# Normalization of v moved to VectorE behind a power on GpSimd, with query weights, biases and loads moved in the order of work (linear attention, then a gated MLP)

## The chip, the cores and the metric

The kernel runs on one core of one Trainium2 chip. The metric is the device time of one execution in microseconds (us), the median of several executions. Five engines work side by side, each through its own queue in its own order, and wait for each other by semaphores: TensorE (PE in the profile; its weight loads are PEld), VectorE (DVE), ScalarE (ACT), GpSimd (POOL) and SyncE (SP, which here only issues DMAs).

## What is computed

The inputs are q, k and v of 8 batches, 8 heads, 576 tokens and 64 elements a head, and the weights of a feature map and of an MLP. Cut to what matters:

```python
def phi(x):                                   # 64 -> 256 features
    proj = einsum('bhsd,df->bhsf', x, w_phi)  # 128 projections
    proj = proj - max(abs(proj), axis=-1)
    return concatenate([exp(proj), exp(-proj)])
kv  = einsum('bhsf,bhsd->bhfd', phi(k), v);  z = sum(phi(k), axis=2)
x   = (phi(q) @ kv) / (phi(q) @ z + 1e-06)    # -> (batch, 576, 512)
h   = maximum(x @ w_in, 0.0);  u, v = h[..., :512], h[..., 512:]
v_n = (v - mean(v)) / sqrt(var(v) + 1e-06)    # over the 512 of a token
v_s = einsum('ts,bsd->btd', w_spatial, v_n) + b_spatial[None, :, None]
out = (u * v_s) @ w_out
```

The normalization of v is the line of `v_n`: a mean and a variance for each token, then one subtraction and one product for each element.

## The kernel before

**Units and batches.** The 576 tokens of a batch are 512 main tokens, four blocks of 128, and a tail of 64; the tails of two batches share a tile. Attention works in 36 units: for each batch four *pair* units (two heads, all main tokens), and for each two batches one *tail* unit (all heads, 128 tail tokens). Unit 2 is the first tail; units 0, 1, 3 and 4 are batch 0, 5 to 8 batch 1, 9 the second tail, 10 to 13 batch 2.

**A unit's stages** are spread over several steps. `a_keys` projects the keys (L267), VectorE takes their absolute maximum `mk` (L279) and ScalarE two exponentials (L282). `a_scale` (L299) scales v by the exponential of the maximum: two products of 128x512 on GpSimd (`vs`, L307) and a small copy; tails do the same into `vst` (`tail_scale`, L317). `a_queries` takes the queries' maxima `mq` (L293) and splits them into two bf16 halves, `mhl` (L296, L297), on VectorE for the first five units and on GpSimd later. `a_max_t` transposes `mhl` (L328), `a_qfeat` projects the queries again, now with the maximum subtracted inside the product, and takes exponentials (L366). From batch 2 on (`merged`, XB = 2) the subtraction sits in the weights: `wm` (L161) holds the projection of each head beside rows of `sel` that pick the head's maximum, and `a_max_t` writes the maxima into free rows of the transposed queries (L331, L332). `a_kv` and `a_num` make the sums and the numerator.

**The MLP** of a batch is a list of tasks (`b_tasks`, L592) that is queued when the batch's attention is done, and is interleaved with later units by `fill` (L620), a given cost per step. `b_v` makes a block of v (L448), ScalarE its relu `vr` (L450), VectorE mean and variance (L451, L452). `root` (L454) takes four small GpSimd instructions: epsilon added, the power -0.5 (`ALU.pow`), mean times that, and the sign. `normalize` (L464) then does one product and one addition with two numbers per token on GpSimd: four times 128x512 a batch (`b_ln`, L481) and once 64x512 for the tail, inside `b_v_tail`. `b_u` makes u, `b_s` (L519) the spatial products with `w_spT` (L524, L525), which VectorE multiplies by u (L527), `b_o` the output. `w_spT` is made once, by transposes of the loaded `wsp`, `wspr` and `wspt` among batch 0's tasks (`transpose_spatial`, L210); after the last of them ScalarE copies the bias from `bsp_row` into two rows of it.

**The order.** A planner places instructions on each engine as their inputs come ready by its own estimate. What is wrapped in `pin` (L60) keeps its place behind what the program has given the same engine just before. The profile names pinned instructions by L61, the line of `pin`. The loop over steps (L713) emits step i's stages and MLP tasks and then what `at(i, ...)` has listed for step i: the loads (k, q and MLP weights from GpSimd's queue, with a cast to bf16; v from SP's), the transposing DMAs of keys and queries (`cross`, on SP, three steps ahead of a unit of batch 2 or later), the copy `q_even`, the tail scaling of batch 1, and `weights_with_max`, which builds `wm` in twelve small GpSimd instructions in steps 6 and 7.

Of the kernel before, what the change touches and what calls it, by code (L numbers as in the profile page):

```python
# [16 lines left out]
def kernel(  # L17
# [162 lines left out]
        pin(nc.scalar.copy)(out=wphi2[r, y * F:(y + 1) * F], in_=wphi_f[r, :])  # L180
    for i in range(2):
        fill_vnt(i, nc.gpsimd.tensor_copy)
    for x in ("k", "q"):
        pin(nc.gpsimd.tensor_copy)(out=half_tile(x, 0, 0)[:, 2:4], in_=first[x, 2])
    load("k", 0, 1, 0, 2)
# [5 lines left out]

    w_in_bf = cpool.tile([P, KC, DFF], BF16)
    w_out_bf = cpool.tile([P, KC, DM], BF16)
    wsp = s2.tile([P, NB, T0], BF16, tag="vn", name="wsp", bufs=2)
    wspr = cpool.tile([P, NB, TL], BF16)
    wspt = s2.tile([TL, S], BF16, tag="ob", name="wspt", bufs=6)
    bsp_row = s2.tile([P, S], FP32, tag="xT", name="bsp_row", bufs=3)
    nc.sync.dma_start(out=bsp_row[TL:TL + 1, :], in_=moe_b_spatial)
# [11 lines left out]
    def transpose_spatial(i):  # L210

        pt = psum.tile([P, S], BF16, tag="bank", name="pt")
        if i < NB:
            sc = POS[i]
            for tp, c in enumerate(POS):
                nc.tensor.transpose(out=pt[:, tp * P:(tp + 1) * P], in_=wsp[:, c, bass.ds(sc, P, step=NB)],
                                    identity=ident)
            nc.tensor.transpose(out=pt[:, T0:S], in_=wspt[:, bass.ds(sc, P, step=NB)],
                                identity=ident[:TL, :TL])
            nc.vector.tensor_copy(out=w_spT[:, i, :], in_=pt)  # L220
            return
        for bl in range(2):
            lo = bl * TL
            for tp, c in enumerate(POS):
                nc.tensor.transpose(out=pt[lo:lo + TL, tp * P:(tp + 1) * P], in_=wspr[:, c, :], identity=ident)
            nc.tensor.transpose(out=pt[lo:lo + TL, T0:S], in_=wspt[:, T0:S], identity=ident[:TL, :TL])
            nc.vector.tensor_copy(out=w_spT[lo:lo + TL, NB + bl, :], in_=pt[lo:lo + TL, :])
        for bl, row in ((0, TL), (1, 0)):
            r = slice(row, row + 1)
            pin(nc.scalar.copy)(  # L230
                out=w_spT[r, NB + bl, 0:T0].rearrange("o (a b p) -> o a b p", a=2, b=2),
                in_=bsp_row[r, 0:T0].rearrange("o (p b a) -> o a b p", a=2, b=2))
            pin(nc.scalar.copy)(out=w_spT[r, NB + bl, T0:S], in_=bsp_row[r, T0:S])


    def merged(u):
        return u["pair"] and u["b"] >= XB

    def weights_with_max(n):
        for j in range(4 * n, 4 * n + 4, 2):  # L240
            pin(nc.gpsimd.tensor_copy)(out=wm[:, j, :], in_=wphi2[:, 0:F])
            pin(nc.gpsimd.tensor_tensor)(out=wm[:, j + 1, :], in0=wphi2[:, F:2 * F], in1=sel[:, j + 1, :], op=ALU.add)
            pin(nc.gpsimd.tensor_copy)(out=wm[D:D + 2 * H, j, :], in_=sel[0:2 * H, j, :])

    def q_even(u):
        u["qE"] = qts[u["i"] % len(qts)]
# [37 lines left out]
    def a_queries(u):  # L284

        m, early = mhl[u["i"] % NM], u["i"] < EARLY
        if not early:
            mq = small.tile([P, H], FP32, tag="mq", name="mq")
        for half in range(2):
            pq = by_token(u["qT"], half)  # L290
            if early and half == 0:
                mq = pq[:, 0, 0:H]
            nc.vector.tensor_reduce(out=mq[:, 4 * half:4 * half + 4], in_=pq, axis=AX.X, op=ALU.max,  # L293
                                    apply_absolute_value=True)
        eng = nc.vector if early else nc.gpsimd
        eng.tensor_copy(out=m[:, 0:H], in_=mq)  # L296
        eng.tensor_tensor(out=m[:, H:2 * H], in0=mq, in1=m[:, 0:H], op=ALU.subtract)  # L297

    def a_scale(u):  # L299
        em = small.tile([P, 2, H], FP32, tag="em" if u["pair"] else "em_t", name="em", bufs=3 if u["pair"] else 1)  # L300
        for s, sc in ((0, -1.0), (1, 1.0)):
            nc.scalar.activation(out=em[:, s, :], in_=u["mk"], func=AF.Exp, bias=0.0, scale=sc)  # L302
        if u["pair"]:
            pj = u["pj"]
            vs = feat.tile([P, 2, H, DA], BF16, tag="vs", name="vs", bufs=4)
            for s in range(2):
                nc.gpsimd.tensor_tensor(out=vs[:, s, :, 0:D], in0=st[u["b"]]["v"][:, pj * H:(pj + 1) * H, :],  # L307
                                        in1=em[:, s, :].unsqueeze(2).to_broadcast([P, H, D]), op=ALU.mult)
            nc.gpsimd.tensor_copy(out=vs[:, :, :, D:DA], in_=em.unsqueeze(3).to_broadcast([P, 2, H, 2]))
            u["vs"] = vs  # L310
        else:
            d = gs[u["g"]]
            d["vs"], d["unit"], d["em"] = vst[u["g"] % 2], u, em
            for bl in range(2 if u["g"] else 1):
                tail_scale(u["g"], bl)
# [135 lines left out]
        nc.vector.bn_stats(out=stats[r], in_=dst[r])  # L451
        nc.vector.bn_aggr(out=mv[r], in_=stats[r])  # L452

    def root(mv, r, n):  # L454

        var = small.tile([P, NB, 1], FP32, tag="var", name="var")
        rs = small.tile([P, NB, 2], FP32, tag="rs", name="rs")
        nc.gpsimd.tensor_scalar(out=var[r, 0:n], in0=mv[r, 0:n, 1:2], scalar1=1e-6, scalar2=None, op0=ALU.add)
        nc.gpsimd.tensor_tensor(out=rs[r, 0:n, 0:1], in0=var[r, 0:n], in1=neghalf[r, 0:n].unsqueeze(2), op=ALU.pow)
        nc.gpsimd.tensor_tensor(out=var[r, 0:n], in0=mv[r, 0:n, 0:1], in1=rs[r, 0:n, 0:1], op=ALU.mult)  # L460
        nc.gpsimd.tensor_scalar(out=rs[r, 0:n, 1:2], in0=var[r, 0:n], scalar1=-1.0, scalar2=None, op0=ALU.mult)
        return rs

    def normalize(dst, src, rs):  # L464
        nc.gpsimd.tensor_scalar(out=dst, in0=src, scalar1=rs[:, 0:1], scalar2=rs[:, 1:2],  # L465
                                op0=ALU.mult, op1=ALU.add)

    def b_v(b, j):
        d = st[b]
        if j == 0:  # L470
            d["vn"] = s2.tile([P, NB, HALF], BF16, tag="vn", name="vn", bufs=2)
            d["mv"] = small.tile([P, NB, 2], FP32, tag="mv", name="mv")
            d["vr"] = {}
        d["vr"][j] = s2.tile([P, HALF], BF16, tag="vr", name="vr", bufs=5)
        stats = small.tile([P, 6], FP32, tag="stats", name="stats")
        v_mm(lambda kc: d["xT"][:, kc, j * P:(j + 1) * P], d["vr"][j], slice(0, P), stats, d["mv"][:, j, :])

    def b_root(b):
        st[b]["rs"] = root(st[b]["mv"], slice(0, P), NB)

    def b_ln(b, j):  # L481
        d = st[b]
        normalize(d["vn"][:, j, :], d["vr"][j], d["rs"][:, j, :])

    def b_v_tail(g, bls):
        d = gs[g]
# [2 lines left out]
        stats = small.tile([P, 6], FP32, tag="stats", name="stats")  # L489
        mv = small.tile([P, 1, 2], FP32, tag="mv_t", name="mv_t")  # L490
        v_mm(lambda kc: d["xTt"][:, kc, r], vr, r, stats, mv[:, 0, :])
        rstd = root(mv, r, 1)
        for bl in bls:
            r = slice(bl * TL, (bl + 1) * TL)
            normalize(vnt[g % 2][r, bl, :], vr[r], rstd[r, 0, :])

    def b_u(b, dc):
        d = st[b]
# [93 lines left out]
    def b_tasks(b):  # L592
# [5 lines left out]
        ss = [(MS, lambda dc=dc: b_s(b, dc)) for dc in range(KC)]  # L598
        ns = [(0.0, lambda j=j: b_ln(b, j)) for j in range(NB)]
        ts = outs[:1] + [(MM, lambda: b_v_tail(g, [bl]))] + vs[:2] + outs[1:2] + vs[2:]  # L600
        ts.append((0.0, lambda: b_root(b)))
        if b == 0:
            ts += [(0.3, lambda i=i: transpose_spatial(i)) for i in range(NB + 1)]
        for y in range(NB):
            ts += ns[y:y + 1] + outs[2 + y:3 + y] + us[y:y + 1]
        ts += [(MM / 2, lambda: b_u_tail(g, [bl]))] + ss
        ts.append((MS / 2, lambda: b_s_tail(g, [bl])))
        return ts + (out_tasks(b) if b == B - 1 else [])
# [70 lines left out]
        io.setdefault(i, []).append(lambda: f(*a))  # L679

    at(1, load_v, 1)
    at(2, load, "k", 1, 0)
    at(2, load, "q", 1, 0)
    at(3, load, "k", 1, 1)
    at(3, load, "q", 1, 1)
    at(4, load_weight, w_in_bf[:, :, HALF:DFF], cols[:, :, HALF:DFF])
    at(4, load_weight, wspt, moe_w_spatial[T0:S, :])
    at(5, tail_scale, 0, 1)
    at(5, load_weight, wsp, rows[:, :, 0:T0])
    at(5, load_weight, wspr, rows[:, :, T0:S])  # L690
    at(6, load_weight, w_in_bf[:, :, 0:HALF], cols[:, :, 0:HALF])
    at(8, load_weight, w_out_bf, moe_w_out.rearrange("(kc p) f -> p kc f", p=P))
    for u in units:
        i = u["i"]
        if not u["pair"] and u["g"] > 0:
            early = 1 if u["g"] > 1 else 0
            at(i - AT - early, load_tail, "k", u["g"])
            for x in ("q", "v"):
                at(i - AT + 1 - early, load_tail, x, u["g"])
        if u["pair"] and u["b"] >= XB:  # L700
            if u["pj"] == 0:
                for n, (x, y) in enumerate((("k", 0), ("q", 0), ("k", 1), ("q", 1))):
                    at((4, 4, 6, 7)[n] if u["b"] == XB else i - AB + n, load, x, u["b"], y)
                for y in range(2):
                    at(i - AB + 1 + 2 * y, load_v, u["b"], y)
            for x in ("k", "q"):
                at(i - XP, cross, x, u)
    at(6, weights_with_max, 0)
    at(7, weights_with_max, 1)
    for u in units:  # L710
        if merged(u):
            at(u["i"] - 1, q_even, u)
# [36 lines left out]
```

## Time and profile before

| what | value |
|---|---|
| median of 3 executions | 283.72 us (282.17 to 284.65) |
| profiled execution, its own time | 284.76 us |
| span of the profiled execution | 282.7 us, 8134 instructions |
| granted TensorE clock, mean | 0.986 |
| `vs` products on GpSimd (L307) | 64, mean 1044 ns, 65.5 us |
| normalization on GpSimd (L465), 128x512 and 64x512 | 32 and 8, mean 766 and 767 ns |
| power on GpSimd (L459), 128x4 and 64x1 | 8 and 8, mean 1046 and 584 ns |
| the other steps of `root` (L458, L460, L461), 128x4 | 236, 203 and 248 ns |
| the same, 64x1 | 239, 186 and 250 ns |
| `wm` on GpSimd: copies of 128x128, additions, copies of 16x128 | 4 each, 297, 426 and 283 ns |
| bias copies on ScalarE, 1x512 and 1x64 | 2 each, 1111 and 238 ns |
| small operations on VectorE: reciprocal 128x4, memset 128x5 | 163 and 62 ns |
| ScalarE copy 128x512 bf16 (L262) | 615 ns |

In a row of busy times by stage the columns are the stage, its length, and for each engine its busy time with the number of instructions, then the granted share of TensorE's clock, the mean busy share of the DMA engines (transfers waiting in a queue count, so it can be over 1) and GB/s. A row of waits gives the engine, its instruction and line, what it waited for, the total, how often, and the longest. A row of the chain gives start, duration, and the instruction. A matmul's duration holds its way through the array; four of 512 columns that follow each other take 0.86 us of the chain.

### The profile page before, as it was taken

What the parts mean: (1) busy time and instruction counts of PE and PEld (TensorE: products, weight loads), DVE (VectorE), ACT (ScalarE), POOL (GpSimd) and SP (SyncE); (2) the same over time, 40 slices, a digit from 0 to 9 for tenths busy, and PEclk for the clock granted to TensorE, in tenths of its full rate; (3) what the DMA queues carried; (4) which work ended last, traced back from release to release, by engine and by line L of the source; (5) the groups of instructions that cost most, each with busy time, mean ns of one, the idle gap of its engine ahead of it and who ended that gap; (6) DMA issues with size and microseconds to landing.
All of it is one profiled execution on the core that took longest, in us unless ns stands there. A gap on an engine that the chain in (4) does not pass through costs nothing.

```text
span 282.7 us, 8134 instructions
## 1 busy us (share of the span) xinstructions
PE 257.1 (91%) x3001; PEld 173.1 (61%) x3042; DVE 231.2 (82%) x576; ACT 219.5 (78%) x499; POOL 200.5 (71%) x362
## 2 busy tenths in 40 slices
PE   2777979986999999999999999999999999999993
PEld 1466866754776667666666775766666765654441
DVE  7979987875799979998889989998889897566341
ACT  5689996978399997899889987899699977723601
POOL 5988999999859886799949974889548832511710
PEclk9979999999799999999999999999999999999999
DMA  7989999999986999989989999999766301120305
GB/s 205 238 205 125 152 144 217 111 164 195 225 87 163 130 243 196 162 206 210 214 96 130 207 252 138 200 214 217 86 122 132 86 2 68 46 77 37 112 3 186
DMA packets 85148, 42.43 MB, mean 150 GB/s; under 512 B 52146, under 2 KB 80498, under 8 KB 85108
## 3 DMA queue, kind: packets, MB, share of 16 engines
q1 hardware_dynamic: 60020, 30.95, 55.0%
q0 software_dynamic: 24928, 10.89, 34.9%
q8 instruction: 24, 0.39, 0.6%
q14 instruction: 16, 0.13, 0.2%
q10 hardware_dynamic: 160, 0.07, 0.1%
HBM read 32.85 MB, written 9.44 MB: 150 GB/s over the span
## 4 chain that ended last, share of the span: by engine, by line
PE 62%; POOL 12%; ACT 9%; DVE 6%; DMA 4%; issue 4%; SPq 0%; POOLq 0%; ACTq 0%; DVEq 0%
PE ps L524 9%; PE pv L448 9%; PE po L549 9%; PE ps L267 6%; PE pu L503 6%; ACT kf L282 5%; PE pv L379 4%; PE pn L399 4%; PE pq L345 3%; DMA q_bf<-in_q_dram 3%; PE ps L525 2%; POOL vs L307 2%; POOL vst L61 2%; DVE stats L451 2%; ACT qf L366 2%
## 5 line engine op out<-in xcount | busy, mean ns | idle before, releaser
L282 ACT ACTIVATE kf<-ps 128x512 bf16<-128x512 f32 x144 | 76.2, 637 | 9.9 <-DVE mk L279 9.5
L307 POOL TENSOR_TENSOR vs<-v_f,em 128x512 bf16<-128x512 f32 x64 | 65.5, 1044 | 19.0 <-ACT em L302 17.6
L366 ACT ACTIVATE qf<-pq 128x512 bf16<-128x512 f32 x128 | 66.6, 620 | 9.6 <-PE pq L345 8.5
L279 DVE TENSOR_REDUCE mk<-ps 128x4 f32<-128x512 f32 x72 | 47.7, 677 | 1.2 <-PE ps L267 0.5
L293 DVE TENSOR_REDUCE mq<-ps 128x4 f32<-128x512 f32 x62 | 39.8, 680 | 2.6 <-PE ps L267 1.4
L524 PE MATMUL ps<-w_spT,vn 128*128 128x512 bf16 x116 | 33.1, 384 | 3.6 <-POOL vn L465 3.1
L527 DVE TENSOR_TENSOR uT<-ps,uT 128x512 bf16<-128x512 f32 x32 | 22.0, 687 | 16.8 <-PE ps L525 16.8
L451 DVE BATCH_NORM_STATS2 stats<-vr 128x6 f32<-128x512 bf16 (+1 forms) x40 | 26.7, 684 | 7.3 <-ACT vr L450 6.9
L549 PE MATMUL po<-w_out_bf,uT 128*128 128x512 bf16 x121 | 32.0, 380 | 0.4
L503 PE MATMUL pu<-xT,w_in_bf 128*128 128x512 bf16 x121 | 31.5, 380 | 0.5 <-issue 0.2
L448 PE MATMUL pv<-w_in_bf,xT 128*128 128x512 bf16 x116 | 30.7, 380 | 0.7
L450 ACT ACTIVATE vr<-pv 128x512 bf16<-128x512 f32 (+1 forms) x40 | 23.5, 615 | 7.6 <-PE pv L448 5.9
L379 PE MATMUL pv<-vs,kf 128*128 128x66 bf16 x512 | 24.3, 194 | 1.3 <-ACT kf L282 1.3
L390 DVE TENSOR_TENSOR x<-pn,rc 128x256 bf16<-128x256 f32 x64 | 24.9, 417 | 0.3
L465 POOL TENSOR_SCALAR vn<-vr,rs 128x512 bf16<-128x512 bf16 x32 | 24.3, 766 | 1.1
L399 PEld LDWEIGHTS <-qf 128*128 128x128 bf16 x512 | 20.5, 99 | 7.1 <-issue 1.4
L505 ACT ACTIVATE uT<-pu 128x512 bf16<-128x512 f32 x32 | 19.7, 641 | 4.9 <-PE pu L503 3.2
L379 PEld LDWEIGHTS <-kf 128*128 128x128 bf16 x512 | 21.8, 97 | 2.5 <-issue 1.5
L552 ACT COPY ob<-po 128x512 f32<-128x512 f32 x18 | 11.0, 614 | 14.9 <-PE po L549 8.4
L399 PE MATMUL pn<-kv,qf 128*128 128x66 bf16 x512 | 22.0, 195 | 0.3 <-ACT qf L366 0.3
L381 PE MATMUL pv<-vst,kf 128*128 128x66 bf16 x128 | 21.2, 192 | 0.0
L524 PEld LDWEIGHTS <-vn 128*128 128x128 bf16 x128 | 11.7, 98 | 13.8 <-POOL vn L465 4.6
(133 smaller groups left out, 572.2 us busy)
## 6 DMA issues: line engine op xcount, KB each, us to landing
out_dram<-ob SPq DMA_DIRECT2D x32, 256.0 KB, 2.5
v_f<-in_v_dram SPq DMA_DIRECT2D x14, 512.0 KB, 7.0
k_bf<-in_k_dram POOLq DMA_DIRECT2D x14, 256.0 KB, 6.3
q_bf<-in_q_dram POOLq DMA_DIRECT2D x14, 256.0 KB, 6.4
qt<-qT_b SPq DMA_DIRECT2D x24, 64.0 KB, 4.2
v_tl<-in_v_dram SPq DMA_DIRECT2D x8, 128.0 KB, 3.4
v_f<-in_v_dram SPq DMA_DIRECT2D x1, 1024.0 KB, 9.4
w_in_bf<-in_moe_w_in_dram POOLq DMA_DIRECT2D x2, 512.0 KB, 10.5
```

Source lines behind the costliest of these rows:

```text
L279: nc.vector.tensor_reduce(out=u["mk"][:, hs], in_=pk, axis=AX.X, op=ALU.max, apply_absolute_value=True)
L282: nc.scalar.activation(out=u["kf"][:, s, hs, :], in_=pk, func=AF.Exp, bias=0.0, scale=sc)
L293: nc.vector.tensor_reduce(out=mq[:, 4 * half:4 * half + 4], in_=pq, axis=AX.X, op=ALU.max, apply_absolute_value=True)
L307: nc.gpsimd.tensor_tensor(out=vs[:, s, :, 0:D], in0=st[u["b"]]["v"][:, pj * H:(pj + 1) * H, :], in1=em[:, s, :].unsqueeze(2).to_broadcast( ...
L366: nc.scalar.activation(out=qf[:, s], in_=pq, func=AF.Exp, bias=0.0, scale=sc)
L379: nc.tensor.matmul(out=pv[:, hh, s, :], lhsT=u["kf"][:, s, 4 * hh + c, :], rhs=u["vs"][:, s, 4 * hh + c, :], start=(c == 0), stop=False)
L399: nc.tensor.matmul(out=pn[:, pos, :], lhsT=u["qf"][hh][:, s, pos, :], rhs=d["kv"][:, 2 * u["pj"] + hh, s, :], start=(s == 0), stop=(s == 1))
L448: nc.tensor.matmul(out=pv[r], lhsT=lhs(kc), rhs=w_in_bf[:, kc, HALF:DFF], start=(kc == 0), stop=(kc == KC - 1))
L451: nc.vector.bn_stats(out=stats[r], in_=dst[r])
L503: nc.tensor.matmul(out=pu, lhsT=w_in_bf[:, kc, dc * P:(dc + 1) * P], rhs=d["xT"][:, kc, :], start=(kc == 0), stop=(kc == KC - 1))
L524: nc.tensor.matmul(out=ps, lhsT=d["vn"][:, sp, cs], rhs=w_spT[:, sp, 0:T0], start=(sp == 0), stop=False)
L549: nc.tensor.matmul(out=po[r], lhsT=lhs(dc), rhs=w_out_bf[:, dc, :], start=(dc == 0), stop=(dc == KC - 1))
```

## The change

- `normalize` runs on VectorE as one instruction (the mean subtracted, then the product with the root), pinned. Epsilon is added on VectorE right after the last statistics (`with_eps`); `root` is then the power alone, on GpSimd, pinned. The product with the mean and the sign are gone.
- Root and normalization are tasks of their own for tail and main blocks. The tail's root comes right behind the last `b_v`, the main blocks' root behind the first `b_u`; the tail's and the first block's normalization come behind the second `b_u`, two more behind the third, the last behind the fourth.
- `wm` is built before step 0, in two ScalarE copies and one GpSimd addition over all heads.
- The four bias copies on ScalarE move from the last `transpose_spatial` to steps 1 and 2.
- Loads: `wsp` and `wspr` become one load of whole rows. The two query loads of batch 2 move from steps 4 and 7 to 7 and 9, the second key load from 6 to 8, its v loads from 5 and 7 to 8 and 9; `wsp` from 5 to 7, `wspt` from 4 to 6, the second half of `w_in` from 6 to 5, `w_out` from 8 to 9; the second tail's loads from 4 and 5 to 5 and 6; batch 3's k and q loads come one step later.
- `mhl`, `vs` and its small copy are pinned.

```diff
+    pin(nc.scalar.copy)(out=alternate(wm, 0), in_=wphi2[:, 0:F].unsqueeze(1).to_broadcast([P, NP, F]))
+    pin(nc.scalar.copy)(out=alternate(wm[D:D + 2 * H], 0), in_=alternate(sel[0:2 * H], 0))
+    pin(nc.gpsimd.tensor_tensor)(out=alternate(wm, 1), in0=alternate(sel, 1),
+                                 in1=wphi2[:, F:2 * F].unsqueeze(1).to_broadcast([P, NP, F]), op=ALU.add)
...
-    wsp = s2.tile([P, NB, T0], BF16, tag="vn", name="wsp", bufs=2)
-    wspr = cpool.tile([P, NB, TL], BF16)
+    wsp = s2.tile([P, NB, S], BF16, tag="vn", name="wsp", bufs=2)
...
-        for bl, row in ((0, TL), (1, 0)):
-            r = slice(row, row + 1)
-            pin(nc.scalar.copy)(
+    def spatial_bias(bl):
+        r = slice(TL, TL + 1) if bl == 0 else slice(0, 1)
+        pin(nc.scalar.copy)(
...
-        eng.tensor_copy(out=m[:, 0:H], in_=mq)
-        eng.tensor_tensor(out=m[:, H:2 * H], in0=mq, in1=m[:, 0:H], op=ALU.subtract)
+        pin(eng.tensor_copy)(out=m[:, 0:H], in_=mq)
+        pin(eng.tensor_tensor)(out=m[:, H:2 * H], in0=mq, in1=m[:, 0:H], op=ALU.subtract)
...
-    def root(mv, r, n):
-        var = small.tile([P, NB, 1], FP32, tag="var", name="var")
-        rs = small.tile([P, NB, 2], FP32, tag="rs", name="rs")
-        nc.gpsimd.tensor_scalar(out=var[r, 0:n], in0=mv[r, 0:n, 1:2], scalar1=1e-6, scalar2=None, op0=ALU.add)
-        nc.gpsimd.tensor_tensor(out=rs[r, 0:n, 0:1], in0=var[r, 0:n], in1=neghalf[r, 0:n].unsqueeze(2), op=ALU.pow)
-        nc.gpsimd.tensor_tensor(out=var[r, 0:n], in0=mv[r, 0:n, 0:1], in1=rs[r, 0:n, 0:1], op=ALU.mult)
-        nc.gpsimd.tensor_scalar(out=rs[r, 0:n, 1:2], in0=var[r, 0:n], scalar1=-1.0, scalar2=None, op0=ALU.mult)
+    def with_eps(mv, r, n):
+        var = small.tile([P, NB, 1], FP32, tag="var", name="var")
+        nc.vector.tensor_scalar(out=var[r, 0:n], in0=mv[r, 0:n, 1:2], scalar1=1e-6, scalar2=None, op0=ALU.add)
+        return var
+
+    def root(var, r, n):
+        rs = small.tile([P, NB, 1], FP32, tag="rs", name="rs")
+        pin(nc.gpsimd.tensor_tensor)(out=rs[r, 0:n], in0=var[r, 0:n], in1=neghalf[r, 0:n].unsqueeze(2), op=ALU.pow)
         return rs
 
-    def normalize(dst, src, rs):
-        nc.gpsimd.tensor_scalar(out=dst, in0=src, scalar1=rs[:, 0:1], scalar2=rs[:, 1:2],
-                                op0=ALU.mult, op1=ALU.add)
+    def normalize(dst, src, mv, rs):
+        pin(nc.vector.tensor_scalar)(out=dst, in0=src, scalar1=mv[:, 0:1], scalar2=rs, op0=ALU.subtract, op1=ALU.mult)
...
-        ts.append((0.0, lambda: b_root(b)))
+        ts.append((0.0, lambda: b_root_tail(g, [bl])))
         if b == 0:
             ts += [(0.3, lambda i=i: transpose_spatial(i)) for i in range(NB + 1)]
-        for y in range(NB):
-            ts += ns[y:y + 1] + outs[2 + y:3 + y] + us[y:y + 1]
+        ns.insert(0, (0.0, lambda: b_ln_tail(g, [bl])))
+        ts += outs[2:3] + us[:1] + [(0.0, lambda: b_root(b))] + outs[3:4] + us[1:2]
+        ts += ns[:2] + outs[4:] + us[2:3] + ns[2:4] + us[3:] + ns[4:]
...
+    at(1, spatial_bias, 0)
+    at(2, spatial_bias, 1)
...
+    at(4, load, "k", 2, 0)
     at(5, tail_scale, 0, 1)
-    at(5, load_weight, wsp, rows[:, :, 0:T0])
-    at(5, load_weight, wspr, rows[:, :, T0:S])
-    at(6, load_weight, w_in_bf[:, :, 0:HALF], cols[:, :, 0:HALF])
-    at(8, load_weight, w_out_bf, moe_w_out.rearrange("(kc p) f -> p kc f", p=P))
+    at(5, load_weight, w_in_bf[:, :, 0:HALF], cols[:, :, 0:HALF])
+    at(5, load_tail, "k", 1)
+    at(6, load_tail, "v", 1)
+    at(6, load_tail, "q", 1)
+    at(6, load_weight, wspt, moe_w_spatial[T0:S, :])
+    at(7, load, "q", 2, 0)
+    at(7, load_weight, wsp, rows)
+    at(8, load, "k", 2, 1)
+    at(8, load_v, 2, 0)
+    at(9, load, "q", 2, 1)
+    at(9, load_v, 2, 1)
+    at(9, load_weight, w_out_bf, moe_w_out.rearrange("(kc p) f -> p kc f", p=P))
...
-    at(6, weights_with_max, 0)
-    at(7, weights_with_max, 1)
```

## The prediction

> **What bounds the kernel now.** I read the totals first, then engine busy time by stage, then who waits for whom in each stage, then the chain.
>
> ```profile
> PE 257.1 (91%) x3001; PEld 173.1 (61%) x3042; DVE 231.2 (82%) x576; ACT 219.5 (78%) x499; POOL 200.5 (71%) x362
> PEclk9979999999799999999999999999999999999999
> ```
>
> No engine is idle enough to be ruled out by its total, so the stages have to be looked at. The second line shows two dips of the granted clock, in the third and the eleventh slice.
>
> ```profile
> core 0: us, PE busy (x) PEld busy (x) DVE busy (x) ACT busy (x) POOL busy (x), PEclk, DMA share, GB/s
> 28.00:77.00 49.00, 42.69 (x567) 31.96 (x571) 38.60 (x104) 39.55 (x93) 46.42 (x86) 0.97 1.31 172
> 105.00:210.00 105.00, 103.76 (x1239) 69.94 (x1257) 95.03 (x225) 91.87 (x214) 80.36 (x145) 1.00 1.10 178
> 210.00:255.00 45.00, 44.02 (x512) 28.21 (x517) 35.56 (x95) 32.71 (x74) 21.98 (x42) 1.00 0.29 68
> 70.20:73.60 3.40, 3.38 (x36) 2.40 (x37) 2.15 (x8) 0.00 (x0) 3.31 (x7) 0.50 1.29 285
> ```
>
> From 28 to 77 us POOL is busy 46.4 of 49 us: it is the bound. From 105 to 210 PE is busy throughout and DVE 95.0 of 105 us. From 210 on only PE is full. The last row is the second dip: 3.4 us at half clock. TensorE's and VectorE's waits tell what those loads mean:
>
> ```profile
> PE ps L524 <- POOL vn L465: 2.4, 2, 1.3
> PE pt L328 <- POOL mhl L297: 1.5, 1, 1.5
> PE ps L267 <- ACT qf L366: 1.1, 1, 1.1
> ...
> DVE uT L527 <- PE ps L525: 4.3, 6, 1.2
> DVE qT_b L331 <- PE pt L328: 2.1, 2, 1.2
> ```
>
> The first three are PE's in 28 to 77, the last two DVE's in 105 to 210, where all of DVE's named waits sum to 8.3 us (4.3+2.1+1.1+0.8). The chain shows what the first row stands for, and the timeline of the end shows it again:
>
> ```profile
> 66.25 0.77 POOL vn L465
> 67.02 0.82 POOL q_bf L61
> 67.90 2.28 POOL vn L465 x3
> 70.22 0.61 PE ps L524
> ...
> 264.56 1.04 POOL L459 TENSOR_TENSOR rs<-var,neghalf 128x4 f32<-128x4 f32 x1
> 266.31 3.02 POOL L465 TENSOR_SCALAR vn<-vr,rs 128x512 bf16<-128x512 bf16 x4
> 267.65 0.63 PE L524 MATMUL ps<-w_spT,vn 128*128 128x512 bf16 x2
> 269.38 0.39 PE L524 MATMUL ps<-w_spT,vn 128*128 128x512 bf16 x1 [0.36 <-POOL vn L465]
> ```
>
> Both times the spatial products stand behind GpSimd's normalization. What the same work may cost on VectorE:
>
> ```profile
> L332 DVE COPY qt<-qT_b x24: 283/285/1564, 77.1 to 239.7; 16x512 bf16<-16x512 bf16 x24
> L465 POOL TENSOR_SCALAR vn<-vr,rs x32: 757/767/796, 66.3 to 268.6; 128x512 bf16<-128x512 bf16 x32
> L451 DVE BATCH_NORM_STATS2 stats<-vr 128x6 f32<-128x512 bf16 x32 | 21.4, 683 | 3.5 <-ACT vr L450 3.1
> ```
>
> The minimum and maximum of the first row matter: the copy of 1564 ns, at 166.71 us, ran while GpSimd did its two `vs` products from 166.07 to 168.12; the copy ended with them.
>
> **The change part by part.** The sums are against the profiled execution (284.76 us, span 282.7); the median of the three runs is 1.04 us lower, and I apply the differences to the median, 283.7.
>
> *Normalization in the middle.* GpSimd loses per batch four products of 0.767, one of 0.767 for the tail and three of four small steps, twice (0.69 and 0.68): 5.2 us. It was not waited for there, so this brings nothing by itself. VectorE gains five normalizations and two additions of epsilon. No row shows this operation on VectorE; 0.285 (the copy of as many bf16 elements in SBUF) and 0.683 (statistics over the same tile) bound it. I take 0.285, since the copy too reads and writes SBUF alone. For the addition the nearest rows are 0.062 (a memset of 128x5) and 0.163 (the reciprocal of 128x4); I take 0.1. That is 5 x 0.285 + 2 x 0.1 = 1.63 us a batch. On top come waits for GpSimd: the 24 copies took 9.7 us where 24 x 0.285 is 6.8, so 0.12 each on average; `vs` and `vst` fill about a third of GpSimd's time there (8 x 1.04 a batch and 2 x 1.04 for the tail, of about 30), which would make a random start wait a third of some 0.9 (half a pair), about 0.3. Between these 0.2: 1.0 us a batch. The normalizations are pinned behind the power on GpSimd (1.05 us, 0.58 for the tail), which stands in GpSimd's order behind `vs` products; if it is late, the `mk` and `mq` reductions queued behind on VectorE are late and with them ScalarE's exponentials: 0 to 1.05 a batch, I take 0.2. Together 2.8 us a batch, against DVE's named idle time of 8.3 us over the 3.5 batches of 105 to 210, 2.4 a batch. So most is absorbed and VectorE is then full. About 4.6 batches lie between 80 and 215 us; I take a loss of 0.5 in each, **+2.3**. Bounds: 0, if idle time takes all, and 4.6 x 2.8 = 13 if none. Later batches cost nothing: DVE has 9.4 of 45 us free from 210 on.
>
> A rule speaks against this part: by the Trainium skill, "SBUF — State Buffer", section Who interferes with whom, a Vector operation that uses two ports and a GpSimd instruction exclude each other for the whole instruction. The row of 1564 ns agrees, the median of 285 says that it seldom happens; by the rule every start into a `vs` pair waits, about 0.3 each, 0.5 a batch more than I take.
>
> *The start.* GpSimd's 46.4 us in 28 to 77 lose the first batch's normalization (5.2) and the twelve instructions for `wm` (4 x 0.426 + 4 x 0.297 + 4 x 0.283 = 4.0), and one load issue (0.74). Of DMA issues the `wspt` (0.56), key tail (1.42) and one q load (0.8) move behind step 4's `vs`, so the scaled maxima `mhl` that PE waits for at 42.8 come earlier: -1.5. With `vn` in time PE's waits of 2.4 go, and with them, I assume, the half clock at 70.2, 3.4 us at half rate: -1.7. The four bias copies (2 x 1.11 + 2 x 0.24 = 2.7) leave ScalarE's queue where PE waited 1.1 for `qf` behind them: -1.1. Sum -6.7. Late next is VectorE, at 38.6 plus some 3 of 49 us.
>
> Given back: the bias copies stand now on ScalarE in steps 1 and 2. There it has 1.15 us free before 14.10, but from 19.63 to 25.8 it runs without a gap, and the second 1.35 us fall in front of that: 0 to 2.7, I take 1.2. In the first step ScalarE's two copies (nearest row 0.615 for 128x512) fit before its first exponential at 7.58; GpSimd's one addition (1.04 by the `vs` row, 1.7 by four times 0.426) waits for the weights, cast until 5.7, and pushes the second pair of key and query casts, behind which stand the next k and q loads: 0 to 0.8, I take 0.1. The loads by need: `wsp` is issued at step 7 instead of 5, the query half of batch 2 at step 7 instead of 4, right before SP's transposing DMA that reads it and blocks SP's queue until it lands. In 28 to 60 the loads took 5.6 to 13.4 us to land, and the matrix is wanted by the transposes from 52.3, the queries at 60.2; with GpSimd at step 7 near 46, `wsp` lands at 52 to 59. Cost 0 to 5, I take 0.6, because `w_in_bf`, whose two loads took up to 14.7 us, now goes ahead of it and most of the clogging transposes come later. Start: -6.7 + 1.9 = **-4.8**, between -7.5 and +1.
>
> *The end.* Stats end at 264.1; then 0.1 for epsilon, 1.05 for the power, 4 x 0.285, with 0.1 between: ready at 266.6. PE reaches the products at 267.65 and ended the first one 1.1 us late (269.83, against 267.65 + 5 x 0.215 = 268.7). So the 2.7 us by which the chain shortens are worth **-1.2** only; PE is next. Bounds -0.8 and -1.6.
>
> Sum: -4.8 + 2.3 - 1.2 = -3.7; 283.7 - 3.7 = 280.0.
>
> **The rivals.** *VectorE becomes the bound* (slower). Mechanism: each of three groups of normalizations a batch meets a `vs` pair and waits 1.0 on average, half its 2.05. Then 1.63 + 3.0 = 4.6 a batch, less the 2.4 of idle time, 2.2 x 4.6 = +10.3; 283.7 - 6.0 + 10.3 = 288.0. It makes the kernel slower from 1.3 us lost a batch on. For: DVE's 95 of 105 us. Against: the median of 285.
>
> *The loads eat the start's gain* (within 1%). `wsp` and the queries come 3.3 us later than PE wants them: 283.7 - 1.5 - 1.2 + 2.3 = 283.3. For: a DMA share of 1.31 in 28 to 77. Against: the same bytes in all, ordered by when they are needed.
>
> *VectorE at the statistics' pace*: the normalization takes 0.683 as the statistics do, 2.0 a batch more; with 0.4 of it absorbed, 1.6 x 4.6 = +7.4, and 0.8 of the end's gain goes: about 288. Then the change doesn't do what it says.
>
> *All absorbed*: the start's -7.5, the end's -1.6, the middle +1: 275.6.
>
> **How the numbers follow.** Forecast 0.40 (own range 277 to 282), all absorbed 0.11, loads 0.20, VectorE bound 0.21, the statistics' pace 0.08. About 1% is what a measurement of this kernel can tell from no change: 280.9 and 286.5. Faster: 0.34 of the forecast, the 0.11 and 0.01 of the loads, 0.46. Within 1%: 0.06, 0.17 and 0.03 of the slow cases, 0.26. Slower: 0.02 and 0.26, 0.28. The range holds eight of ten from 274 to 289: both bounds of the start, up to 2.3 a batch in the middle.
>
> **What would show it.** Right: normalization at about 0.285 us on DVE with a few over 1 us; no PE wait for `mhl` at 42; no half clock near 70; DVE at 97% or more in the middle; PE at the last products without a wait. Wrong: PE waiting for `wsp` or `qT_b` between 50 and 62; named DVE idle time still over 2 us a batch beside a longer batch period (the vn groups at 97.3 and 245.5 are five batches, 29.6 each); DVE standing before a normalization for the power.

## The result, and the profile after

The changed kernel takes 293.83 us (291.11 to 294.82, four executions), the kernel before 282.95 in the same comparison: a ratio of 1.036, 95% interval 1.027 to 1.045. It is slower, where the prediction said 280.0 and gave up to 289. The profiled execution took 293.95 us, its span is 292.2, 9.5 more than before. In what follows a median holds all executions of a kernel, and a ratio leaves out one slow execution each of E4, E5 and E11.

First the totals and the granted clock of the changed kernel, from its page:

```profile
PE 262.8 (90%) x3042; PEld 174.2 (60%) x3042; DVE 246.2 (84%) x632; ACT 221.6 (76%) x501; POOL 155.6 (53%) x262
PEclk9979999999899999999799999999999999999998
```

GpSimd has lost 44.9 us of work (200.5 to 155.6) and VectorE gained 15.0. No engine is over 90%, so the totals don't say where the time went; the stages and the waits have to. The clock dips three times now ahead of the end, in the third, eleventh and twentieth slice. Next the same stages as in the prediction, and behind them the third dip:

```profile
core 0: us, PE busy (x) PEld busy (x) DVE busy (x) ACT busy (x) POOL busy (x), PEclk, DMA share, GB/s
28.00:77.00 49.00, 42.99 (x579) 32.02 (x577) 41.22 (x112) 37.29 (x90) 37.71 (x62) 0.97 1.20 173
105.00:210.00 105.00, 99.77 (x1182) 66.22 (x1179) 95.84 (x241) 88.16 (x205) 60.93 (x104) 0.98 1.11 175
210.00:255.00 45.00, 43.52 (x547) 28.93 (x546) 40.10 (x108) 35.93 (x83) 15.69 (x29) 1.00 0.30 73
...
139.85:143.26 3.41, 3.41 (x24) 1.86 (x23) 3.27 (x10) 1.56 (x4) 0.00 (x0) 0.50 1.05 179
```

GpSimd is no longer the bound of the first stage. From 105 to 210 TensorE is busy for 99.8 of 105 us where it was 103.8, yet VectorE, which was to be full there, does 95.8, hardly more than the 95.0 before. So something holds VectorE. The waits of VectorE, GpSimd and TensorE name it:

```profile
DVE vn L61 <- POOL rs L61: 8.0, 5, 2.6
...
POOL vs L61 <- ACT em L305: 69.9, 26, 5.9
...
PE pu L516 <- DVE x L393: 2.0, 1, 2.0
PE ps L270 <- DVE xT L417: 1.9, 1, 1.9
...
PE pt L223 <- DMA wsp<-in_moe_w_spatial_dram: 1.9, 1, 1.9
```

VectorE stands 8.0 us before normalizations for the power (`rs`). GpSimd, with its new free time, stands 69.9 us for `em`, the exponential that scales the values (17.6 before). TensorE's waits follow: twice about 2 us for VectorE, and 1.9 for the spatial matrix. One such place in the timeline, first GpSimd, then VectorE, then TensorE (start, duration, instruction, idle time before it and what ended it):

```profile
131.04 0.83 POOL L61 DMA_DIRECT2D k_bf<-in_k_dram  x1
135.00 2.04 POOL L61 TENSOR_TENSOR vs<-v_f,em 128x512 bf16<-128x512 f32 x2 [3.12 <-ACT em L305]
136.99 0.20 POOL L61 CAST vs<-em 128x32 bf16<-128x32 f32 x1
137.15 1.04 POOL L61 TENSOR_TENSOR rs<-var,neghalf 128x4 f32<-128x4 f32 x1
```

```profile
131.03 0.17 DVE L459 TENSOR_SCALAR var<-mv 128x4 f32<-128x4 f32 x1
...
135.16 0.41 DVE L393 TENSOR_TENSOR x<-pn,rc 128x256 bf16<-128x256 f32 x1
138.22 0.41 DVE L61 TENSOR_SCALAR vn<-vr,mv,rs 128x512 bf16<-128x512 bf16 x1 [2.65 <-POOL rs L61]
138.55 0.39 DVE L392 RECIPROCAL rc<-pn 128x4 f32<-128x4 f32 x2
138.97 0.42 DVE L393 TENSOR_TENSOR x<-pn,rc 128x256 bf16<-128x256 f32 x1
```

```profile
139.45 1.54 PE L516 MATMUL pu<-xT,w_in_bf 128*128 128x512 bf16 x4 [2.02 <-DVE x L393]
```

The variance is ready at 131.2 and GpSimd idle from 131.9. The power could run then and be done by 133. But in GpSimd's order it stands behind a scaling `vs` of a later unit, which waits for its exponential until 135.0, and that pair takes 2.04 us more. The power ends at 138.2. VectorE has come to its normalization at 135.6 and stands; behind it in its own order is the `x` that TensorE waits for. TensorE is idle for 2.02 us, and the half clock begins 0.4 us after that gap. Two waits at the heads of two queues are in series here: from 131.9 to 135.0 GpSimd is idle while VectorE works, and from 135.6 to 138.2 VectorE is idle while GpSimd does the scaling and then the power.

The normalization itself, and the end:

```profile
L61 DVE TENSOR_SCALAR vn<-vr,mv,rs x32: 394/409/930, 68.3 to 277.5; 128x512 bf16<-128x512 bf16 x32
L61 DVE TENSOR_SCALAR vnt<-vr,mv_t,rs x8: 392/406/436, 64.5 to 276.1; 64x512 bf16<-64x512 bf16 x8
```

```profile
274.18 0.18 DVE L455 BATCH_NORM_AGGREGATE mv<-stats 128x2 f32<-128x6 f32 x1
...
274.71 1.01 POOL L61 TENSOR_TENSOR rs<-var,neghalf 128x4 f32<-128x4 f32 x1 [2.72 <-DVE var L459]
...
276.54 1.38 DVE L61 TENSOR_SCALAR vn<-vr,mv,rs 128x512 bf16<-128x512 bf16 x4
...
278.22 1.03 PE L537 MATMUL ps<-w_spT,vn 128*128 128x512 bf16 x4
```

One takes 0.409 us, between the 0.285 and the 0.683 of the prediction's bounds. At the end the chain from the last statistics to the last normalized block takes 3.6 us (274.36 to 277.92). It took 5.3 before (264.08 to 269.33), and 2.5 were predicted; a copy of `ob` (275.36 to 276.05) and the tail's normalization on VectorE go first. It is short enough: TensorE reaches its products with no wait.

To see where the time goes, I compare when ScalarE begins the first key exponential of a unit, and VectorE the last batch's products with u, in the profiled executions. The differences to the kernel before, in us (+ is later; the kernels E1 to E10 are those of the next section):

| mark, at us before | after | E1 | E3 | E9 | E10 |
|---|---|---|---|---|---|
| third unit, 14.1 | +2.4 | +1.4 | +1.2 | +2.0 | +2.4 |
| 44.7 | 0.0 | +0.1 | -1.2 | -0.4 | +0.1 |
| 77.1 | +1.4 | -0.1 | -1.6 | -0.2 | -0.8 |
| 109.2 | +4.0 | +0.1 | -0.5 | +0.9 | -0.8 |
| 135.0 | +7.7 | +0.1 | -0.1 | +1.6 | -0.7 |
| 167.2 | +9.8 | +0.1 | +2.1 | +8.1 | -0.7 |
| 227.6 | +10.6 | +0.7 | +2.8 | +10.2 | -0.2 |
| last products, 270.1 | +9.5 | +0.4 | +1.7 | +9.1 | -1.3 |

At 45 us the change is level with the kernel before. It is 1.2 us behind E3 there, though nothing has waited for a power yet, so single profiles of the start differ by that much for other reasons. From there it falls further behind E3, which was edited in the place of the power alone, in three steps of 1.8, 1.5 and 3.3 us (at the marks 77.1, 109.2 and 135.0), and each follows a stand of VectorE for the power, at 65.7, 101.3 and 135.6. The three make 6.6 of the 7.8 us between the two spans. The last row gives back 1.1.

### The profile page after: what moved, and what is told of

It is laid out like the page before. It is cut to its first block, busy times and chain, and to the rows that moved or that the text cites. A ratio compares the mean times of both kernels' runs of the same rounds, so it can differ in the third digit from the quotient of the medians.

```text
span 292.2 us, 8087 instructions
## 1 busy us (share of the span) xinstructions
PE 262.8 (90%) x3042; PEld 174.2 (60%) x3042; DVE 246.2 (84%) x632; ACT 221.6 (76%) x501; POOL 155.6 (53%) x262
## 4 chain that ended last, share of the span: by engine, by line
PE 54%; DVE 11%; ACT 9%; DMA 9%; POOL 8%; issue 4%; SPq 4%; ACTq 0%; POOLq 0%
PE ps L537 9%; PE pv L451 8%; PE po L562 8%; ACT kf L285 5%; PE pu L516 5%; PE ps L270 4%; POOL vs L61 4%; PE pv L382 4%; SPq L61 4%; DVE mk L282 3%; PE pn L402 3%; PE ps L538 2%; PE pq L348 2%; DMA v_f<-in_v_dram 2%; DMA wsp<-in_moe_w_spatial_dram 2%
## 5 line engine op out<-in xcount | busy, mean ns | idle before, releaser
L61 POOL TENSOR_TENSOR vs<-v_f,em 128x512 bf16<-128x512 f32 x64 | 65.5, 1040 | 72.2 <-ACT em L305 69.9
L537 PE MATMUL ps<-w_spT,vn 128*128 128x512 bf16 x128 | 34.7, 389 | 0.9 <-DVE vn L61 0.9
L516 PE MATMUL pu<-xT,w_in_bf 128*128 128x512 bf16 x128 | 32.6, 384 | 2.0 <-DVE x L393 2.0
L451 PE MATMUL pv<-w_in_bf,xT 128*128 128x512 bf16 x128 | 31.4, 379 | 0.9 <-ACT kf L285 0.6
L61 POOL TENSOR_TENSOR rs<-var,neghalf 64x1 f32<-64x1 f32 (+1 forms) x16 | 12.7, 795 | 29.8 <-DVE var L459 22.9
L565 ACT COPY ob<-po 128x512 f32<-128x512 f32 x18 | 11.0, 610 | 14.1 <-PE po L562 8.7
L61 POOL TENSOR_TENSOR vst<-v_tl,em 64x512 bf16<-64x512 f32 x16 | 16.3, 1038 | 8.7 <-ACT em L305 8.5
```

Source lines behind the costliest of these rows:

```text
L61: return lambda *a, **kw: tc.keep_in_program_order(start(*a, **kw))
L451: nc.tensor.matmul(out=pv[r], lhsT=lhs(kc), rhs=w_in_bf[:, kc, HALF:DFF], start=(kc == 0), stop=(kc == KC - 1))
L516: nc.tensor.matmul(out=pu, lhsT=w_in_bf[:, kc, dc * P:(dc + 1) * P], rhs=d["xT"][:, kc, :], start=(kc == 0), stop=(kc == KC - 1))
L537: nc.tensor.matmul(out=ps, lhsT=d["vn"][:, sp, cs], rhs=w_spT[:, sp, 0:T0], start=(sp == 0), stop=False)
```

## The experiments

My theory after the comparison: the larger part is VectorE standing for a power that is late in GpSimd's order; the smaller is VectorE's own added work. Rivals: the added work is the whole; or the other parts of the change (pins, loads, biases) are.

**E1, normalization back on GpSimd, the rest of the change kept.**

```diff
-        pin(nc.vector.tensor_scalar)(out=dst, in0=src, scalar1=mv[:, 0:1], scalar2=rs, op0=ALU.subtract, op1=ALU.mult)
+        nc.gpsimd.tensor_scalar(out=dst, in0=src, scalar1=rs[:, 0:1], scalar2=rs[:, 1:2], op0=ALU.mult, op1=ALU.add)
...
```

> The changed kernel with the normalization, epsilon, the four steps of the root and their place among the tasks back on GpSimd as before; the rest of the change (weights with maxima, biases, loads, pins) kept. If the normalization is what cost the middle (VectorE standing behind the power, or VectorE's extra 1.9 to 2.3 us a batch): the shift grows no more after the first three batches, the end loses its 1.1 us again, and the time falls by some 8 to 284 to 286 us. If the other parts carry it (pins, late loads, biases): 291 to 294 us, as the changed kernel.

Measured: 285.02 us, ratio to before 1.001 (0.997 to 1.005). With the normalization on GpSimd the rest of the change is worth nothing in sum; the loss comes with the normalization's part (epsilon, power, normalization and their tasks).

**E2, the normalization's part alone, on the kernel before.** Epsilon, power, normalization and their tasks as in the change; nothing else.

> The kernel before with only the normalization moved to VectorE: epsilon, the pinned power, the pinned normalization and their tasks. If the normalization is the cause: some 8 to 9 us over the kernel before from 100 to 250 us, less 1.1 at the end, so 289 to 292 us, and VectorE stands 2 to 2.7 us before single normalizations for the power. If the middle's loss comes from the other parts: within 2 us of the kernel before, 281 to 285 us.

Measured: 296.86 us, ratio 1.042 (1.036 to 1.048). VectorE stands 8.8 us for the power, up to 2.9. By the ratios this part alone costs some 1.6 us more than the whole change, by the medians 3.0, but the two intervals overlap: that the rest of the change helps it isn't shown yet.

**E3, the power early.** The main blocks' power moves from behind the first `b_u` to right behind the tail's power.

```diff
         ts.append((0.0, lambda: b_root_tail(g, [bl])))
+        ts.append((0.0, lambda: b_root(b)))
...
-        ts += outs[2:3] + us[:1] + [(0.0, lambda: b_root(b))] + outs[3:4] + us[1:2]
+        ts += outs[2:3] + us[:1] + outs[3:4] + us[1:2]
```

> The changed kernel with the main blocks' power right behind the tail's, ahead of the first block of u, so that GpSimd takes it ahead of the scaling of a later unit that waits for its exponential. If VectorE's standing behind the late power is the cause: the waits of 2.0 to 2.65 us go (VectorE's wait for the power under 1.5 us in all instead of 8.0), the second dip of the clock near 140 us goes, and the time falls by 5 to 7 to 287 to 289 us. If VectorE's load is the cause, the waits may go but the time stays within 1.5 us of the changed kernel, 292 to 295 us; a power that is itself pinned ahead of the scaling and waits for the variance would delay the scaling instead, and give 294 to 296 us.

Measured: 286.16 us, ratio 1.005 (1.001 to 1.009). The wait for the power falls from 8.0 to 0.2 us, and 7.7 us of the time are gone with one task moved. GpSimd at the place shown above:

```profile
126.85 1.01 POOL L61 TENSOR_TENSOR rs<-var,neghalf 128x4 f32<-128x4 f32 x1 [0.20 <-DVE var L459]
127.82 0.84 POOL L61 DMA_DIRECT2D k_bf<-in_k_dram  x1
130.56 2.04 POOL L61 TENSOR_TENSOR vs<-v_f,em 128x512 bf16<-128x512 f32 x2 [1.91 <-ACT em L305]
```

The power now runs ahead of the scaling, in time in which GpSimd would have been idle, and the scaling waits for its exponential all the same. The third dip of the clock is gone too; whether the dip was part of the loss, E4 tells below.

**E5, the power where it was, but nothing waits for it.** The normalization multiplies by a constant; the division by the deviation is left out.

```diff
-        pin(nc.vector.tensor_scalar)(out=dst, in0=src, scalar1=mv[:, 0:1], scalar2=rs, op0=ALU.subtract, op1=ALU.mult)
+        pin(nc.vector.tensor_scalar)(out=dst, in0=src, scalar1=mv[:, 0:1], scalar2=neghalf[rs, 0:1], op0=ALU.subtract, op1=ALU.mult)
...
```

> The changed kernel, but the normalization multiplies by a constant in place of the root of this token's variance (the division by the deviation is left out of the result). The power is still made where it was, in the same place of GpSimd's order, and VectorE has the same instructions in the same order; only nothing waits for the power. If standing behind the power is the cause of the larger part: VectorE's 8.0 us of waits for it are gone, and the time falls to 285 to 288 us, as with the power placed early (286.2). If the early power helped by other things (GpSimd's order, the scaling of the keys' values coming sooner): it stays at 291 to 294 us.

Measured: 286.54 us, ratio 1.006 (1.003 to 1.010), as E3. Both kernels' intervals lie around the same value, though GpSimd's order is the change's in one and altered in the other. So it is the wait, and not another effect of moving the power on GpSimd. VectorE's order is not quite the one that was expected to stay: in two batches, at 65 and at 135 us, the planner put the first normalizations a few places earlier, in E5, E3 and E12 alike. At the stand between these, at 101.3 us, VectorE's order is the change's in all of them, and E3 gains its 1.5 us there all the same.

**E12, the power not pinned**, all else as in the change.

```diff
-        pin(nc.gpsimd.tensor_tensor)(out=rs[r, 0:n], in0=var[r, 0:n], in1=neghalf[r, 0:n].unsqueeze(2), op=ALU.pow)
+        nc.gpsimd.tensor_tensor(out=rs[r, 0:n], in0=var[r, 0:n], in1=neghalf[r, 0:n].unsqueeze(2), op=ALU.pow)
```

> The changed kernel with one edit: the power is not pinned, so that the planner may put it on GpSimd ahead of a scaling whose exponential is not there yet; tasks, the normalization's pin and all else stay. If the fixed place of the power is the cause: VectorE's 8.0 us of waits for it go and the time is near that of the early power, 286 to 288 us. If the planner puts it no earlier, since its tasks come late or its estimate has the exponential ready: 291 to 294 us.

Measured: 287.99 us, ratio 1.013 (1.008 to 1.019). The planner, left free, puts the power ahead of the waiting scaling. Most of the loss goes, so it is the fixed place that costs, not the task's position in the list alone.

**E6, every normalization twice, with the early power.**

```diff
-        pin(nc.vector.tensor_scalar)(out=dst, in0=src, scalar1=mv[:, 0:1], scalar2=rs, op0=ALU.subtract, op1=ALU.mult)
+        for _ in range(2):
+            pin(nc.vector.tensor_scalar)(out=dst, in0=src, scalar1=mv[:, 0:1], scalar2=rs, op0=ALU.subtract, op1=ALU.mult)
```

> The changed kernel with the early power, and every normalization done twice in a row with the same result: 40 more instructions on VectorE, by the row of the changed kernel 0.394 to 0.41 each, 2.0 us a batch. If VectorE has become the bound of the middle, the whole of it is paid in the 4.3 batches from 105 to 230 us and in the last: +8 to +10, so 294 to 297 us against 286.2. If VectorE still has room and the middle's 4.4 us lie in something else: +0 to +3, 286 to 289 us.

Measured: 302.54 us, ratio 1.064 (1.057 to 1.071): 16.4 us over E3, where I expected at most 10. VectorE's busy total rises by 19.1 us (247.5 to 266.6), so a microsecond more on VectorE costs 0.86 on average over the kernel. E3's row from 105 to 210, and E6's:

```profile
105.00:210.00 105.00, 102.13 (x1204) 68.45 (x1221) 98.83 (x247) 90.03 (x208) 61.47 (x108) 1.00 1.09 176
```

```profile
105.00:210.00 105.00, 97.07 (x1134) 63.65 (x1148) 101.00 (x250) 84.99 (x197) 60.05 (x104) 0.98 1.07 170
```

VectorE goes from 98.8 to 101.0 of 105 us, TensorE falls from 102.1 to 97.1. In E3 neither is full, but beyond E3 nearly the whole of any further work on VectorE is paid.

**E7, the early power without the rest of the change**: the kernel before with E2's part and E3's move.

> The kernel before with only the normalization on VectorE and with the power early; weights, biases, loads and pins as before. If the rest of the change is worth nothing in sum, as the run with the normalization back on GpSimd says (1.0009 of before): 285 to 288 us. If the rest helps once GpSimd is free of the normalization: 289 to 291 us; if it hurts then: 281 to 283 us.

Measured: 295.08 us, ratio 1.039 (1.033 to 1.044). None of my three outcomes: with VectorE's work moved and the power early, the rest of the change is worth some 9 us, though E1 says that it is worth nothing when the normalization is on GpSimd. What of the rest it is, the next two kernels asked.

**E8, the loads at the steps of the kernel before, with the early power.** In E3, the spatial matrix goes back to step 5, the first queries of batch 2 to step 4, and so on; the matrix stays one load.

> The changed kernel with the early power, and the loads at the steps of the kernel before (the spatial matrix at step 5 in place of 7, the first queries of batch 2 at 4 in place of 7; the matrix stays one load). If the late matrix cost the start its gain: TensorE's wait of 2.0 us for it near 51 us goes and the marks from 62 us on come 1 to 2 us earlier, 284 to 285.5 us against 286.2. If something else is as late there (scaled maxima, queries, the loads' traffic in the way of the transposing DMAs): 286 to 288 us.

Measured: 286.17 us, ratio 1.008 (1.004 to 1.011), as E3. The order of the loads makes no difference that shows. TensorE's wait for the matrix is gone in this kernel, and nothing is gained by it.

**E9, E3 without the pins of the scaling and of the maxima's split.**

```diff
-        pin(eng.tensor_copy)(out=m[:, 0:H], in_=mq)
-        pin(eng.tensor_tensor)(out=m[:, H:2 * H], in0=mq, in1=m[:, 0:H], op=ALU.subtract)
+        eng.tensor_copy(out=m[:, 0:H], in_=mq)
+        eng.tensor_tensor(out=m[:, H:2 * H], in0=mq, in1=m[:, 0:H], op=ALU.subtract)
...
-                pin(nc.gpsimd.tensor_tensor)(out=vs[:, s, :, 0:D], in0=st[u["b"]]["v"][:, pj * H:(pj + 1) * H, :],
+                nc.gpsimd.tensor_tensor(out=vs[:, s, :, 0:D], in0=st[u["b"]]["v"][:, pj * H:(pj + 1) * H, :],
...
-            pin(nc.gpsimd.tensor_copy)(out=vs[:, :, :, D:DA], in_=em.unsqueeze(3).to_broadcast([P, 2, H, 2]))
+            nc.gpsimd.tensor_copy(out=vs[:, :, :, D:DA], in_=em.unsqueeze(3).to_broadcast([P, 2, H, 2]))
```

> The changed kernel with the early power, and without the pins of the scaling and of the scaled maxima's split, so that the planner orders these on GpSimd; weights, biases and loads stay as in the change. If these pins make the difference between the early power with the rest of the change (286.2) and without it (295.1): GpSimd takes a split that waits for VectorE's maxima ahead of a ready scaling again, a power behind them is late, and the time is 292 to 296 us. If the difference comes from the weights built early or the biases: 286 to 288 us.

Measured: 292.87 us, ratio 1.031 (1.025 to 1.037): 6.7 us over E3. Most of that lies between 135 and 167 us (+1.6 to +8.1). GpSimd and TensorE there:

```profile
159.81 0.18 POOL L299 CAST mhl<-mq 128x8 bf16<-128x8 f32 x1 [3.64 <-DVE mq L296]
160.08 0.20 POOL L300 TENSOR_TENSOR mhl<-mq,mhl 128x8 bf16<-128x8 f32 x1
160.58 0.79 POOL L61 DMA_DIRECT2D k_bf<-in_k_dram  x1 [0.31 <-issue]
161.39 2.05 POOL L310 TENSOR_TENSOR vs<-v_f,em 128x512 bf16<-128x512 f32 x2
...
163.74 1.66 POOL L61 TENSOR_TENSOR rs<-var,neghalf 64x1 f32<-64x1 f32 x2
165.61 2.18 POOL L310 TENSOR_TENSOR vs<-v_f,em 128x512 bf16<-128x512 f32 x2 [0.21 <-ACT em L305]
```

```profile
168.60 0.38 PE L382 MATMUL pv<-vs,kf 128*128 128x66 bf16 x4 [2.69 <-DVE mq L296]
```

Here it is the split of the maxima that stands at the head of GpSimd's queue, 3.64 us, for a VectorE that is late; behind it stand a scaling pair and the powers. TensorE then waits 2.69 us, and within that wait, at 167.5 us, a stretch of 6.83 us at half clock begins, the 24th slice:

```profile
PEclk9979999799999999999999959999999999999999
```

At half rate such a stretch is worth up to 3.4 us, an estimate, and no run parts it from the wait; E7 has one of the same length at 167.7 us. So the pins are the part of the rest that helps, 6.7 of the 8.9 us: with them the scaling goes first. Read from these lines, it is the same mechanism with another instruction in front.

**E4, the bias copies back behind the last transpose**, all else as in the change.

> The changed kernel with the four bias copies back behind the last transpose of the spatial matrix, as before. If ScalarE's wait of 2.3 us for the bias row's transfer cost what the unit marks show (2.4 us at the third unit): units 2 to 7 come 1.4 to 2.4 us earlier; where they were regained by the eighth unit nothing is left of it at the end, 292 to 295 us. If the early loss runs through to the end: 291 to 292 us.

Measured: 294.89 us, ratio 1.032 (1.023 to 1.041), no different from the change. The third unit comes 1.9 us earlier than in the change (+0.4 instead of +2.4), but at the fourth the kernel is as late as the change (+2.1 and +2.2): ScalarE's 2.3 us for the bias row are replaced by 2.7 us for TensorE. In these first 20 us TensorE waits for the loads of q and k in any case (2.5 us here, 2.1 before).

This profile also tells what the half clock near 140 us was worth. VectorE stands 2.65 us for the power at the same place, and TensorE has the same gap of 2.02 us, ending at 140.46; but no dip follows it, the 20th slice is at full clock:

```profile
PEclk9999999989999999999999999999999999999999
```

From the mark at 109.2 to the one at 135.0 it loses 3.7 us on the kernel before (+5.0 to +8.7), as the change does (+4.0 to +7.7). So the stand costs that without the dip; by the next mark, at 141.3, the change has lost another 0.5 us against E4.

**E10, VectorE only where it pays.** E3 with batches 0 and 7 normalized on VectorE and batches 1 to 6 on GpSimd as before. **E11** is the same with the spatial matrix at step 6 and its last rows at step 7.

```diff
+    ON_DVE = (0, B - 1)
...
-        st[b]["rs"] = root(st[b]["var"], slice(0, P), NB)
+        st[b]["rs"] = root(st[b]["var"], slice(0, P), NB) if b in ON_DVE else root_gp(st[b]["mv"], slice(0, P), NB)
...
```

> The changed kernel with the early power, where only batches 0 and 7 are normalized on VectorE; batches 1 to 6 go back to GpSimd in the manner of the kernel before. If the middle's loss is VectorE's load and the two ends' gains (1.6 at the start, 1.1 at the end) are the normalization's: both gains stay and the middle costs nothing, 281 to 283 us. If the start's gain is given back by the middle's GpSimd order, or the end's gain depends on what lies ahead: 284 to 286 us, as before.

> The same as the one with batches 0 and 7 alone on VectorE, with the spatial matrix loaded at step 6 and its last rows at step 7 (the change has them the other way round). If the late matrix costs the start 2 us: TensorE's wait for it near 51 us goes, and the time is 1 to 2 us lower than the other's. If what comes behind it (maxima, queries, transposing DMAs) is late anyway: within 0.5 us of the other.

Measured: E10 282.71 us, ratio 0.995 (0.992 to 0.998), E11 283.56, ratio 0.996 (0.993 to 0.999). E10 beats both kernels; against before it is half a per cent, less than the 1% named in the prediction, but its interval leaves 1 out. Its middle (E10, 105 to 210) is that of the kernel before, TensorE busy for 104.4 of 105 us:

```profile
105.00:210.00 105.00, 104.41 (x1260) 69.82 (x1259) 96.17 (x225) 91.61 (x212) 80.09 (x145) 1.00 1.13 177
```

So the middle's loss in E3 (+4.4 from 77 to 228 us) is the normalization of the batches 1 to 6. In E11 TensorE's wait for the matrix is gone (2.7 us in E10), but the time is not lower. The predicted 1 to 2 us did not come.

## Why the prediction was wrong

**Standing behind the power.** This is the step that failed: "0 to 1.05 a batch, I take 0.2". It allowed the power's own duration at most. E3 and E5 put it at 7.7 and 7.3 us by their medians (8.9 and 8.5 by the ratios to before, since the chips differ). The bound was false since it left out what stands ahead of the power: the scaling pair of 2.04 us, and above all the wait of that pair for its exponential, 3.12 us in the place shown. The trace of before had the sign: GpSimd's scalings waited 17.6 us for `em` while GpSimd was 71% busy. With 45 us of work taken off GpSimd this waiting grew to 69.9 us (24.1 in E1, where the normalization is on GpSimd), and the change put the power behind it. A freed engine is not free for an instruction that its order keeps back. The prediction had named "DVE standing before a normalization for the power" among the signs that it is wrong; that sign showed, 8.0 us in five places.

**VectorE's work in the middle.** +2.3 was taken, E3 shows +4.4 between the marks at 77 and 228 us. The mechanism was right in the main: idle time absorbs part (VectorE's named waits from 105 to 210 us fall from 8.3 to 4.5 us in E3), and the rest is paid, though VectorE is busy for 94% there and not the 97% that was to show it. The size was off: 0.285 for one normalization should have been 0.409; 5 x 0.124 is 0.62 us a batch, 2.9 over the 4.6 batches, which more than fills the gap of 2.1. The copy was the wrong neighbour. E6 shows the price of still more work, 0.86 per microsecond.

**Waits for GpSimd's scaling** were put at 1.0 us a batch. In E3 the 40 normalizations take 20.0 us instead of 40 x 0.409 = 16.4, so 0.45 a batch. My slower rival, VectorE as the bound through waits of 1.0 for the scaling in each group, was right in its sign and in the engine, but not in what it waits for. The rival at the statistics' pace falls with the 0.409, and "all absorbed" with E3, whose middle is 4.4 us longer though VectorE stands only 0.2 us for the power. The rule of the Trainium skill, "SBUF — State Buffer", section Who interferes with whom, says that when a VectorE instruction in a two-port mode meets one on GpSimd, whichever issues first has the shared ports for its whole instruction. E3 agrees: of eight normalizations that overlap a scaling, five took 0.80 to 1.58 us; three took 0.40 to 0.43, of which one began ahead of the scaling and two within the last 0.25 us of one. None of the other 32 took over 0.45.

**The start.** -4.8 was predicted. In the change the mark at 77 us is 1.4 late, in E3 1.6 early. Of these 3.0 us 1.2 were there at 45 us; the other 1.8 are the power again (VectorE stood 2.52 us at 65.7). The listed waits did shrink: 1.5 for `mhl` and 1.1 for `qf` to at most 0.5, 2.4 for `vn` to 0.6. What took their place is named in the waits: 1.9 us for the spatial matrix, priced at 0.6 with the queries. E8 and E11 took that wait away and got nothing for it, so the rival of the loads names a wait that is there, but not the one that sets the start. What holds the start at about -1 then isn't settled. The marks there differ by 1 to 4 us between kernels with the same first steps (third unit +1.2 in E3, +2.4 in E10), by when the first loads land, so single profiles don't resolve it. The half clock near 70 us, assumed gone for -1.7, stayed in the change (71.6); in E3 it is gone, but there is one at 53.4.

**The bias copies** were priced at +1.2. E4 shows 0: the 2.3 us for the bias row lie beside late loads, and by 45 us the change is level with before.

**The end.** -1.2 predicted; the last two rows of the table give -1.1 in the change, in E3 and in E10. The size is right because TensorE is next, as it was said; the chain itself shortened by 1.7 us and not by 2.7, which happened not to matter.

Sum in the same order: +7.7 for the power (taken: +0.9 within the +2.3), +4.4 for VectorE's work, -1.6 for the start as E3 has it, -1.1 for the end: +9.4, against 9.5 of the spans and 10.9 of the medians. The last three are E3's own distance from the kernel before, 1.7 us by the spans, so the sum confirms the split no further than E3 and E5 do.

## What to carry to other kernels

When work moves to another engine and a small step stays behind, look at what stands ahead of that step in its engine's order, and what that waits for: the bound of the new wait is this wait plus all the work ahead, not the small step's own duration. Taking load off an engine with a fixed order buys waiting at its head unless the order changes too. Where the receiving engine is nearly full, move only the instances that lie on the path, here the first and the last batch of eight.

## What the runs showed of the hardware that was not expected

- A subtraction and a product with two numbers per token on VectorE, bf16 in SBUF, takes 0.409 us for 128x512 where a copy of as many elements per partition took 0.285; back to back, four take 1.38 us.
- The same part of a kernel is worth more or less by its surroundings: the pins and the rest of the change are worth 0 with the normalization on GpSimd (E1), and about 9 us with it on VectorE (E7 against E3).
- Half-clock stretches ahead of the end are 3.41 us long, or 6.83 in E6, E7, E8, E9 and E11, and where they fall moves: at 17.0, 71.6 and 139.9 us in the change, at 53.4 in E3, only at 16.3 in E10 apart from the end. The one at 139.9 began 0.4 us after an idle gap of TensorE of 2.02 us. The Trainium skill, "TensorE: Matmul & The Clock Gate", section Why this matters for your kernels, warns of gaps of more than about 3 us; here a shorter one was followed by a dip, and in E2 three gaps of 1.84 to 2.17 us were, 1.0 to 1.6 us after they ended. In E4 the same gap of 2.02 us was not followed by one, so such a gap alone doesn't decide it.
